# Stacked single-pass score products, decay factors spread by TensorE, and a new order list in a fused mLSTM and gated-MLP kernel

## The chip, the cores and the metric

The kernel runs on one core of one Trainium2 chip. The metric is the device time of one execution in microseconds (us), lower is better; of several executions the median counts. The engines are named as the profile names them: PE is TensorE's matmul, PEld its load of the stationary operand (the weights), DVE is VectorE, ACT is ScalarE, POOL is GpSimd, and SPq is the queue of SyncE, which here issues every DMA.

## The reference

The computation is a gated recurrent attention followed by two gated MLPs, all in fp32.

```python
B, H, S, D = 2, 8, 768, 40
for t in range(S):                                   # per batch and head
    m_new = max(f[t] + m, i[t]); f_stab = exp(f[t] + m - m_new); i_stab = exp(i[t] - m_new); m = m_new
    C = f_stab * C + i_stab * outer(v[t], k[t]);  n = f_stab * n + i_stab * k[t]
    y[t] = sigmoid(o[t]) * (C @ q[t]) / max(|n . q[t]|, 1)
x = y as [1536, 320]
x = ((x @ w_a) * (x @ w_b)) @ w_out                  # 320 -> 1536 -> 320
h = x @ w_in; out = (h * sigmoid(h)) @ w_out2        # 320 -> 2048 -> 320
```

## The kernel before, in words

**Attention.** The recurrence is cut into 12 units `u0` to `u11`: unit u is chunk c = u // 2 of 128 steps of batch b = u % 2, with all eight heads. In a unit, `scores` (parts `s0`, `s1`, four heads each) multiplies keys by queries on TensorE into a PSUM bank. The keys stand block-diagonally in `kz` (three heads of 40 rows in 120 partitions, zeros elsewhere, two buffers used in turn), so that one matmul of 120 rows against the query tile `qT` gives one head. The operands are plain fp32, and the trace shows each such matmul as two MATMUL and two LDWEIGHTS instructions.

`decays` (part `d0`) turns the forget factors, which must stand in all 128 partitions, into the triangle of decay products by a VectorE scan. In units 0 and 1 the factors are spread over the partitions by TensorE: `factors` (parts `f0`, `f1`) multiplies a column of the identity, broadcast to 128 columns, by the gate rows in `scratch`, four fp32 matmuls a part, into PSUM. In units 2 to 11, `load_fs` (parts `l2.e` and so on) reads them instead from a DRAM copy `fsd`, with a broadcasting DMA that writes 512 KB. `weigh` (`w0`, `w1`) multiplies scores by decays on VectorE, `values` (`v0`, `v1`) multiplies the result by the values on TensorE, `carried` (`car`) adds the chunk state, `update` (`upd`) with `adv_in`, `adv_old`, `adv_end` moves the state forward, and `da` to `xl` make the unit's MLP input columns in `xring`. For units below `BUSY` = 6 the state goes through six ScalarE activations and a memset a unit (`ai0` to `ai2`, `ao0` to `ao2`, `az`).

**Weights.** Twelve tiles of the first MLP (`w0` to `w11`) come as 64-bit floats in two DMAs each into a ring of four raw buffers, are narrowed on ScalarE and VectorE (`ap`, `as`, `ao`, `bp`, `bs`, `bo`), and are split into a rounded fp32r half (copies on ScalarE: `ha`, `hb`, `t0`, `t1`) and a rest (subtractions on GpSimd by the helper `rest`: `la`, `lb`, `u0`, `u1`). The tail halves cross partitions by two small DMAs (`v0`, `v1`). The second MLP's sixteen tiles (`x0` to `x15`) are made later.

**MLPs.** `first_layer` makes a hidden tile from eight fp32r matmuls of 256, 384 or 512 columns, `second_layer` three matmuls of 320 columns a unit. Passes `m0` to `m10` are the first MLP, in eleven pieces of (block of units, range of weight tiles), and `n0` to `n2` the second. A hidden tile goes through parts `a`, `b` (TensorE), `e` (eviction, ScalarE), `g` (product, VectorE, or silu, ScalarE), `h` (rounded half, ScalarE), `l` (rest, GpSimd) and `c` (TensorE).

**Order.** The string `ORDER` names every part once; the kernel runs through it, and each part appends its instructions to its engine's queue. So the list fixes the order on each engine and on SPq, each of which works strictly in its own order and waits on semaphores for data and for free buffers. Parts `f0` to `f29` are fillers, four small bf16 matmuls each on the identity (`warm`).

```python
    def scores(n):
        s = bank(f"s_u{u}", P, 4, C)
        for i in range(4):
            g, j = SLOT[4 * n + i]
            nc.tensor.matmul(out=s[:, i], lhsT=kz[u % 2][:, j, g], rhs=un["q", u][:, g], start=True, stop=True)
```

Of the kernel before, what the change touches and what calls it, by code (L numbers as in the profile page):

```python
# [32 lines left out]
lf zeros const li run0 run1 expi0 f26 f3 f8 expf0 f1 pg0 lw0.b l0.t f10 f2 f6 lw0.a w0.ap w0.bp w0.bs w0.bo w0.as  # L33
u1.f0 u0.f1 u0.f0 u0.d0 w0.t1 expf1 w0.hb l0.q l1.k l0.k u0.s0 l1.q f27 f25 l1.t u1.s0 u1.s1 lw2.b lw1.b w0.ao
starts u0.sv sel f13 w0.u1 lw2.a w0.t0 w0.u0 l2.q lw1.a w0.v0 w0.v1 w0.ha w0.la u0.d1 u1.sv u0.sk w0.lb u1.d0 f22
f16 u1.f1 u1.d1 u1.sk f28 f17 u0.s1 f15 f7 f23 f29 f21 expi1 u0.w1 f4 u0.si f12 u0.sig u1.si u0.v1 w1.bp w2.bs w1.bs
w1.bo u1.sig w2.bp u1.az w1.t1 w1.u1 w1.t0 w1.u0 w1.hb w1.lb u0.w0 u0.v0 w2.as w2.bo w2.hb f20 u0.cb f9 w2.t0 w2.u0
w2.t1 w2.ap u1.w1 u1.v1 u1.w0 prod u0.da u0.dn u1.v0 u1.cb u1.upd u1.ai1 u1.ai2 f24 u0.upd u1.ai0 u0.ai0 u1.da
u0.ai2 w2.ao u0.om w2.u1 u0.rc u0.ox u0.xt u0.ai1 w2.ha u1.dn u1.rc u1.om u1.ox w2.lb u1.xt lw5.a lw3.b pg1 u3.si
u2.ao0 l2.e u2.d0 w1.as w1.ap w1.ao u0.px u0.xh l2.k f5 f11 f18 u2.s1 u2.s0 f0 u1.px u2.si u2.car f14 u1.xh w1.ha  # L40
u2.ao1 l2.t u2.sk u2.sv u2.upd u2.w1 u2.v1 w3.bs w2.v0 l4.q lw3.a u0.az u2.ai1 u1.xl l3.e w1.v0 u0.xl w2.la m0.2.a
w3.bp w3.as u2.ai0 u2.w0 u2.v0 u2.cb w2.v1 m0.2.b w1.la u2.az w3.bo w3.hb w3.t1 w3.u1 w3.lb u3.az u3.d0 l3.k l3.q
u3.car u3.s1 u2.sig u2.cc m0.2.e m0.2.g w3.t0 u2.ai2 u2.om w3.ap w3.ao u3.cb u2.da u2.dn u2.rc m0.0.a u2.ao2 m0.0.b
m0.0.e m0.0.g w3.u0 l3.t u3.sk u3.s0 u3.w0 w1.v1 m0.1.b lw4.b w4.bs w4.bp m0.2.h w4.bo m0.1.a u3.sv u3.v0 m0.2.l
u3.w1 u3.v1 u2.ox m0.0.h m0.0.l m0.0.c w3.ha w4.t0 w4.u0 w4.t1 w4.u1 w4.hb w4.lb m0.1.e m0.1.g u3.cc u2.xt u2.px
w3.v0 lw4.a w4.as u3.upd l4.k l5.q w4.ap w4.ao u3.da u3.dn w3.la m0.3.a u3.sig u3.om u3.rc u3.ox lw5.b w5.bp w5.bs
w5.bo m0.3.e lw6.a m0.2.c w3.v1 m0.3.b m0.3.g u2.ae u4.car u4.cb u3.xt w4.ha l5.t u3.ai0 u3.px w4.v0 w4.la m0.4.a
w5.t0 u3.ai2 m0.3.h m0.3.l m0.3.c u3.xh u3.xl m0.1.h w4.v1 m0.4.b l5.k l5.e u5.d0 u3.ai1 m0.4.e m0.4.g m0.1.l m0.1.c
w5.u0 u4.s1 w5.t1 w5.u1 u2.xh u2.xl m1.0.b lw6.b w6.bp u4.si w6.bs m0.4.h m0.4.l m0.4.c u3.ao0 w5.hb w6.bo w6.hb
w6.lb w6.t0 w6.u0 w6.t1 w6.u1 u5.si l4.e u4.d0 l4.t lw7.b u4.sk u3.ao1 m1.0.a m1.0.e m1.0.g u3.ao2 m0.z1 u4.s0 u4.w0  # L50
w7.bp w7.bs w7.bo m1.1.a m1.1.e w5.lb m1.4.a lw8.b w8.bp w8.bs u5.s0 u5.sk u5.w0 w8.bo u5.s1 m1.1.b m1.1.g u4.w1
u5.w1 u3.ae u4.sv u4.v0 m1.0.h m0.z0 u5.car u5.cb u4.v1 u4.cc u5.sv u5.v1 w5.v1 w6.v1 w6.v0 w5.v0 w7.hb w8.hb w7.lb
l7.k w7.t0 w7.u0 u4.az w8.t0 m1.4.e w8.u0 w8.v0 lw9.b w7.t1 w7.u1 m1.1.h m1.1.l w8.t1 w8.lb w8.u1 w8.v1 w6.ap u5.sig
u5.v0 u5.cc u5.om w6.as w6.ao m1.4.b u4.upd m1.1.c m1.3.a u4.sig u5.da u5.dn lw10.b l6.q w7.v1 lw11.b u5.rc u4.da
# [36 lines left out]
m10.0.l y2.px y2.xh y2.xl m10.3.a m9.11.c m9.z0 lx2 x2.p x2.s x2.o x2.h x3.ho x3.lo x2.t x2.l x2.ho x2.lo m10.2.a
# [38 lines left out]
def tile_mlstm_gated_mlps(ctx: ExitStack, tc: tile.TileContext, i_gate, f_gate, q_cols, k_cols, kvo, w1, w2,  # L130
# [149 lines left out]
    def rest(eng, out_, x, hi):  # L280
        return eng.tensor_tensor(out=out_, in0=x, in1=hi.bitcast(F32), op=ALU.subtract)  # L281
# [575 lines left out]
```

## Time and profile before

| | |
|---|---|
| median of 3 runs | 464.43 us (463.83 to 472.82) |
| profiled execution: time / span | 465.23 us / 463.5 us |
| mean granted TensorE clock | 0.996 |
| PE busy | 454.5 us (98%), 3103 instructions |
| PEld / DVE / ACT / POOL busy | 435.9 / 160.7 / 219.1 / 239.2 us |
| DMA | 42.30 MB, mean 91 GB/s |

The profile covers one execution. Busy time is the time in which an engine ran an instruction, as a sum and as a share of the span. Matmuls overlap in the pipeline, so the time that a matmul costs is read from the distance of the starts of a run of them, not from its own duration (277 ns for a score matmul whose neighbours start every 112 ns).

### The profile page before, as it was taken

Reading aid. Unit: us, or ns where it says so; the run is one execution under the profiler, and the core shown is the slowest. Engines: PE = TensorE matmul, PEld = TensorE weight load, DVE = VectorE, ACT = ScalarE, POOL = GpSimd, SP = SyncE. Lnnn points to the kernel's source line nnn. Section 1 sums busy time; section 2 is a strip of 40 time slices with the busy share of each in tenths; the row PEclk is TensorE's granted clock in tenths of the full one; section 3 lists DMA queues with packets and bytes.
Section 4 is the critical chain, followed back from the end, with each engine's and each line's share of the span. In section 5 each row is a group of like instructions: output and inputs, shape, how many; then the busy total and the mean of one; then the engine's idle time right before and its main releaser. Section 6 shows DMA issues by size and latency. Waiting matters only on the chain.

```text
span 463.5 us, 7966 instructions
## 1 busy us (share of the span) xinstructions
PE 454.5 (98%) x3103; PEld 435.9 (94%) x3103; DVE 160.7 (35%) x268; ACT 219.1 (47%) x507; POOL 239.2 (52%) x278
## 2 busy tenths in 40 slices
PE   7999999999999999999999999999999999999996
PEld 6999999999999999999999999999998989998996
DVE  7876665252435465335442342314300000000000
ACT  4867777756421230232553565656634332443333
POOL 5667795666643465152443557468733343332433
PEclk9989999999999999999999999999999999999999
DMA  7887928351003241231233132133001000010001
GB/s 241 286 243 209 311 88 263 106 177 54 1 9 114 51 141 43 85 106 64 93 102 117 64 100 89 63 126 124 2 0 58 0 2 0 1 42 1 0 16 57
DMA packets 25089, 42.30 MB, mean 91 GB/s; under 512 B 2156, under 2 KB 18348, under 8 KB 25052
## 3 DMA queue, kind: packets, MB, share of 16 engines
q1 hardware_dynamic: 25052, 41.80, 28.4%
q8 instruction: 24, 0.39, 0.4%
q14 instruction: 13, 0.11, 0.1%
HBM read 38.99 MB, written 2.02 MB: 88 GB/s over the span
## 4 chain that ended last, share of the span: by engine, by line
PE 88%; DMA 7%; ACT 1%; DVE 1%; issue 1%; SPq 1%; POOL 0%; POOLq 0%; ACTq 0%
PE h L643 46%; PE acc L654 10%; PE acc L652 10%; PE acc L653 10%; PE y_u L491 4%; PE s_u L478 3%; DMA raw_j<-in_w_dram 3%; DMA e_u<-fsd 2%; PE px_u L614 1%; PE ups_u L511 1%; DMA w_j<-tl_j 1%; PE y_u L501 1%; DMA qT_u<-in_q_cols_dram 1%; DVE e_u L453 0%; SPq L230 0%
## 5 line engine op out<-in xcount | busy, mean ns | idle before, releaser
L643 PE MATMUL h<-xring,w_j 128*128 128x256 f32 (+2 forms) x1088 | 179.3, 317 | 0.1
L643 PEld LDWEIGHTS h<-xring,w_j 128*128 128x128 f32 x1088 | 161.9, 190 | 5.0 <-DMA w_j<-tl_j 0.3
L281 POOL TENSOR_TENSOR g2w<-gw,g2w 128x512 fp32r<-128x512 f32 x48 | 63.2, 1323 | 85.7 <-ACT g2w L688 83.7
L281 POOL TENSOR_TENSOR g<-g,g 128x256 fp32r<-128x256 f32 (+1 forms) x60 | 56.0, 941 | 66.6 <-ACT g L688 65.2
L281 POOL TENSOR_TENSOR w_j<-cvt_j,w_j 128x320 fp32r<-128x320 f32 (+3 forms) x72 | 62.6, 877 | 30.7 <-ACT w_j L342 13.1
L643 PE MATMUL h<-xeven,w_j 128*128 128x512 f32 x256 | 62.6, 392 | 0.0
L654 PE MATMUL acc<-w_j,g2w 128*128 128x320 f32 x192 | 59.4, 309 | 0.1
L652 PE MATMUL acc<-w_j,g2w 128*128 128x320 f32 x192 | 59.4, 310 | 0.0
L653 PE MATMUL acc<-w_j,g2w 128*128 128x320 f32 x192 | 59.3, 309 | 0.0
L688 ACT CAST g<-g 128x256 fp32r<-128x256 f32 (+1 forms) x60 | 26.6, 448 | 68.0 <-DVE g L682 46.1
L643 PEld LDWEIGHTS h<-xeven,w_j 128*128 128x128 f32 x256 | 47.1, 188 | 8.8
L684 ACT ACTIVATE gw<-h 128x512 f32<-128x512 f32 x48 | 28.5, 596 | 55.2 <-PE h L643 45.1
L682 DVE TENSOR_TENSOR g<-a,h 128x256 f32<-128x256 f32 (+1 forms) x60 | 28.2, 472 | 75.6 <-PE h L643 45.7
L652 PE MATMUL acc<-w_j,g 128*128 128x320 f32 x144 | 45.5, 316 | 0.0
L688 ACT CAST g2w<-gw 128x512 fp32r<-128x512 f32 x48 | 29.8, 621 | 32.4 <-PE acc L654 31.9
L654 PE MATMUL acc<-w_j,g 128*128 128x320 f32 x144 | 44.7, 310 | 0.3 <-POOL g L281 0.3
L653 PE MATMUL acc<-w_j,g 128*128 128x320 f32 x144 | 44.4, 308 | 0.0
L653 PEld LDWEIGHTS acc<-w_j,g2w 128*128 128x128 f32 x192 | 36.0, 188 | 1.0
L652 PEld LDWEIGHTS acc<-w_j,g2w 128*128 128x128 f32 x192 | 36.1, 188 | 1.0
L674 ACT ACTIVATE a<-h 128x256 f32<-128x256 f32 (+1 forms) x60 | 24.9, 423 | 25.6 <-PE h L643 24.8
L654 PEld LDWEIGHTS acc<-w_j,g2w 128*128 128x128 f32 x192 | 36.0, 188 | 0.4 <-POOL g2w L281 0.4
L281 DVE TENSOR_TENSOR xeven<-px_u,xeven 128x384 fp32r<-128x384 f32 x8 | 4.5, 557 | 68.5 <-ACT xeven L621 68.5
(100 smaller groups left out, 595.9 us busy)
## 6 DMA issues: line engine op xcount, KB each, us to landing
raw_j<-in_w_dram SPq DMA_DIRECT2D x16, 704.0 KB
raw_j<-in_w_dram SPq DMA_DIRECT2D x12, 512.0 KB
kvo_u<-in_kvo_dram SPq DMA_DIRECT2D x12, 480.0 KB
raw_j<-in_w_dram SPq DMA_DIRECT2D x12, 448.0 KB
e_u<-fsd SPq DMA_DIRECT2D x10, 512.0 KB
qT_u<-in_q_cols_dram SPq DMA_DIRECT2D x12, 180.0 KB
kz<-in_k_cols_dram SPq DMA_DIRECT2D x36, 60.0 KB
out_dram<-osb SPq DMA_DIRECT2D x12, 160.0 KB
```

Of the source, the lines that this page charges most:

```text
L281: return eng.tensor_tensor(out=out_, in0=x, in1=hi.bitcast(F32), op=ALU.subtract)
L478: nc.tensor.matmul(out=s[:, i], lhsT=kz[u % 2][:, j, g], rhs=un["q", u][:, g], start=True, stop=True)
L491: nc.tensor.matmul(out=T["y1"][:, h], lhsT=un["e", u][:, h], rhs=T["v"][:, h], start=True, stop=True)
L501: nc.tensor.matmul(out=y2[:, GH[g] + lo:GH[g] + G], lhsT=un["q", u][:, g], rhs=cb[:, g, lo:G], start=True, stop=True)
L643: nc.tensor.matmul(out=po, lhsT=w[:, wi * P:(wi + 1) * P], rhs=xt[:, :, xi], start=(n == 0), stop=(n == len(pairs) - 1))
L652: nc.tensor.matmul(out=o, lhsT=hi, rhs=w[:, off:off + DM], start=first, stop=False)
L653: nc.tensor.matmul(out=o, lhsT=hi, rhs=w[:, off + DM:off + 2 * DM], start=False, stop=False)
L654: nc.tensor.matmul(out=o, lhsT=lo, rhs=w[:, off:off + DM], start=False, stop=last)
L674: nc.scalar.activation(out=A[j], in_=A.pop(("p", j)), func=ACT.Copy, scale=WS ** -2)
L682: nc.vector.tensor_tensor(out=Q[j], in0=A.pop(j), in1=PB.pop(j), op=ALU.mult)
L684: nc.scalar.activation(out=Q[j], in_=PB.pop(j), func=ACT.Silu, scale=1 / WS)
L688: nc.scalar.copy(out=G2[j][:, 0], in_=Q[j])
```

## The change

1. **Stacked scores from unit 4 on** (`PLAIN = 4`). Instead of `kz`, `load_stack` fetches queries and keys (`l4.sq`, `l4.sk`, ...) into raw buffers of the weight ring in a stacked layout of 120 partitions: 40 rows of a head, its first 24 rows again, the 40 rows again, and its last 16 rows again, for nine head slots side by side (four DMAs each, 553 KB in all). `stack_high` (`hq`, `hk`) rounds each to fp32r into a two-buffer tag shared with `kz`, and `stack_low` (`lq`, `lk`) replaces 40 rows by the rests. One fp32r matmul a head then sums the three products high x low, low x high and high x high. `qT` is still loaded for `carried`; the `kz` loads of these units go.
2. **Decay factors of units 2 to 5 spread by TensorE** (`FB = 3`): they get `f0`, `f1`, `d0`, `d1` as units 0 and 1, and their four `load_fs` go.
3. **State updates**: the ScalarE form goes; units 0 to 5 use the forms of the later units, one masked multiplication on VectorE (`am`) and one on GpSimd (`ao`). `ig` moves to another pool.
4. **A new order list**, with a mark behind some parts that names the engine (`:v` VectorE, `:p` GpSimd). Of the parts of passes `m`, 31 `l` go to VectorE, 24 `e` to VectorE, 21 `h` to GpSimd and 10 `h` to VectorE; some 50 other copies, subtractions and products move as well. All 30 fillers stay; they now stand ahead of the first MLP tile.

```diff
@@ ORDER
-lf zeros const li run0 run1 expi0 f26 f3 f8 expf0 f1 pg0 lw0.b l0.t f10 f2 f6 lw0.a w0.ap w0.bp w0.bs w0.bo w0.as
...
+li lf const f29 f25 f16 f5 f22 f23 f28 zeros f10 run0 run1 expf0 expi0 pg0 f0 f4 lw0.a w0.as lw0.b f14 l1.t l0.t
...
+l4.q u3.s1 lw4.b w4.bp w3.bo w4.bs w4.bo u2.da u2.dn u2.rc w2.v0 m0.2.a w2.v1 m0.2.e w4.t1 w4.u1:v w4.t0 w4.u0 w3.hb
...
+n2.14.g n2.14.h n2.14.l n2.14.c n2.12.g n2.12.h n2.12.l n2.12.c n2.2.g n2.2.h n2.2.l n2.2.c n2.z0 n2.z1 n2.z2 n2.z3
@@
-    BUSY = 6
+    PLAIN = 4
+    FB = 3
@@
-    kz = [cat.tile([GR, G, G, C], F32, name=f"kz{i}") for i in range(2)]
+    def keys(dtype, name):
+        return at.tile([P, G * G * C], dtype, tag="kz", name=name)[0:GR].rearrange("p (j g t) -> p j g t", j=G, g=G)
+
+    kz = [keys(F32, f"kz{i}") for i in range(2)]
+    STACK = ((0, 0, D), (D, 0, KT - D), (KT, 0, D), (KT + D, KT - D, D))
+
+    def load_stack(u, x):
+        b, c, s = place(u)
+        t = raws.tile([P, G * G * C], F32, tag="raw", name=f"st{x}_u{u}")[0:GR]
+        un["st", u, x] = t.rearrange("p (j g t) -> p j g t", j=G, g=G)
+        src = (q_cols, k_cols)[x][b, c].rearrange("(j d) g t -> d j (g t)", j=G)
+        for row, lo, hi in STACK:
+            nc.sync.dma_start(out=t[row:row + hi - lo].rearrange("p (j x) -> p j x", j=G), in_=src[lo:hi])
@@
-    def rest(eng, out_, x, hi):
-        return eng.tensor_tensor(out=out_, in0=x, in1=hi.bitcast(F32), op=ALU.subtract)
+    how = {}
+
+    def copy(out_, in_):
+        e = how.get("e", "a")
+        if e == "a":
+            nc.scalar.copy(out=out_, in_=in_)
+        else:
+            (nc.vector if e == "v" else nc.gpsimd).tensor_copy(out=out_, in_=in_)
+
+    def both(out_, x, y, op):
+        (nc.vector if how.get("e") == "v" else nc.gpsimd).tensor_tensor(out=out_, in0=x, in1=y, op=op)
+
+    def rest(out_, x, hi):
+        both(out_, x, hi.bitcast(F32), ALU.subtract)
@@ chunk
         def factors(n):
-            if c > 0:
+            if c >= FB:
                 return
...
+        def stack_high(x):
+            T["sh", x] = keys(F32R, f"sh{x}_u{u}")
+            copy(T["sh", x], un["st", u, x])
+
+        def stack_low(x):
+            r = slice(x * KT, x * KT + D)
+            rest(T["sh", x][r], un["st", u, x][r], T["sh", x][r])
+
         def scores(n):
             s = bank(f"s_u{u}", P, 4, C)
+            T["s", n] = s
+            if u >= PLAIN:
+                for i in range(4):
+                    g, j = SLOT[4 * n + i]
+                    nc.tensor.matmul(out=s[:, i], lhsT=T["sh", 1][:, j, g], rhs=T["sh", 0][:, j, g],
+                                     start=True, stop=True)
+                return
...
-        def adv_old_all():
+        def adv_old():
             gbu = gb[:, b * G:(b + 1) * G, c:c + 1].to_broadcast([GR, G, G * DV])
...
-            if u < BUSY:
-                d.update(az=adv_zero, **{f"ai{j}": lambda j=j: adv_in(j) for j in range(G)})
-            else:
-                d.update(am=adv_mask)
+            d.update(am=adv_mask)
@@ mlp
-            nc.scalar.activation(out=A[j], in_=A.pop(("p", j)), func=ACT.Copy, scale=WS ** -2)
+            pa = A.pop(("p", j))
+            if how.get("e", "a") == "v":
+                nc.vector.tensor_scalar(out=A[j], in0=pa, scalar1=WS ** -2, scalar2=None, op0=ALU.mult)
+            else:
+                nc.scalar.activation(out=A[j], in_=pa, func=ACT.Copy, scale=WS ** -2)
@@ order
         for t in ORDER:
+            t, _, e = t.partition(":")
+            how.clear()
+            if e:
+                how["e"] = e
             parts[t]()
```

## Rows read from the trace of the kernel before

**Rows 1.** The page's first part: busy time, share of the span, instructions.

```profile
PE 454.5 (98%) x3103; PEld 435.9 (94%) x3103; DVE 160.7 (35%) x268; ACT 219.1 (47%) x507; POOL 239.2 (52%) x278
```

**Rows 2.** Busy time by stretch: start and end, length, each engine (instructions), clock, DMA.

```profile
0.00:34.00 34.00, 30.35 (x290) 29.63 (x291) 26.41 (x44) 22.22 (x55) 20.41 (x40) 0.95 0.82 257
34.00:70.00 36.00, 34.23 (x280) 33.17 (x279) 24.00 (x39) 26.26 (x74) 29.64 (x39) 1.00 0.65 201
70.00:452.00 382.00, 382.00 (x2490) 366.08 (x2490) 110.28 (x186) 167.00 (x373) 185.63 (x199) 1.00 0.21 67
```

**Rows 3.** PE in order of time: start, length, line, operation, count, idle before.

```profile
3.43 1.89 PE L425 MATMUL warm<-idb 128*128 128x128 bf16 x16 [3.43 <-DVE idb L727]
14.42 1.11 PE L444 MATMUL fb_u<-scratch,ident 128*128 128x128 f32 x8
15.36 0.61 PE L425 MATMUL warm<-idb 128*128 128x128 bf16 x8
33.80 1.20 PE L643 MATMUL h<-xring,w_j 128*128 128x256 f32 x8
70.50 1.20 PE L643 MATMUL h<-xring,w_j 128*128 128x256 f32 x8
78.55 6.00 PE L643 MATMUL h<-xring,w_j 128*128 128x256 f32 x48
84.39 0.31 PE L652 MATMUL acc<-w_j,g 128*128 128x320 f32 x1
```

**Rows 4.** Stretches of 2 us and one of 10, columns as in group 2.

```profile
24.00:26.00 2.00, 2.00 (x13) 1.72 (x12) 0.49 (x1) 0.84 (x3) 1.84 (x4) 0.50 0.73 218
28.00:38.00 10.00, 9.32 (x91) 9.12 (x91) 9.19 (x12) 7.86 (x22) 5.89 (x8) 1.00 0.98 278
36.00:38.00 2.00, 1.32 (x12) 1.14 (x11) 2.00 (x3) 1.53 (x6) 1.85 (x2) 1.00 0.90 257
62.00:64.00 2.00, 1.31 (x11) 1.11 (x10) 1.22 (x2) 1.75 (x4) 2.00 (x3) 1.00 0.14 33
```

**Rows 5.** The chain that ended last: start, length, what.

```profile
28.07 7.02 DMA e_u<-fsd
77.30 0.22 PE warm L425 x4
129.25 0.90 PE s_u L478 x8
148.77 0.82 PE y_u L491 x8
163.82 0.33 PE px_u L614 x3
183.65 11.17 PE h L643 x64
456.96 1.33 POOLq L852
```

**Rows 6.** Groups by line and form: busy, mean ns of one, idle before.

```profile
L478 PE MATMUL s_u<-qT_u,kz 120*128 120x128 f32 x192 | 25.1, 277 | 0.7 <-DVE e_u L485 0.7
L293 ACT CAST w_j<-cvt_j 128x512 fp32r<-128x512 f32 x12 | 7.4, 619 | 2.1 <-DVE cvt_j L276 2.1
L281 POOL TENSOR_TENSOR w_j<-cvt_j,w_j 128x512 fp32r<-128x512 f32 x12 | 15.4, 1290 | 6.9 <-ACT w_j L293 6.9
L682 DVE TENSOR_TENSOR g<-a,h 128x384 f32<-128x384 f32 x24 | 13.3, 553 | 39.4 <-PE h L643 23.5 <-ACT a L674 10.1 <-POOL g L281 4.0
L528 DVE TENSOR_TENSOR cn_u<-ups_u,bmask 120x369 f32<-120x369 f32 x4 | 2.1, 532 | 0.1
```

**Rows 7.** VectorE and GpSimd in order of time, about 225 us.

```profile
225.06 1.01 POOL L281 TENSOR_TENSOR g<-g,g 128x384 fp32r<-128x384 f32 x1 [0.88 <-ACT g L688]
225.12 1.70 DVE L256 SCALAR_TENSOR_TENSOR cvt_j<-raw_j,cvt_j 128x704 uint32<-128x704 uint32 x1
227.29 0.89 DVE L256 SCALAR_TENSOR_TENSOR cvt_j<-raw_j,cvt_j 128x704 uint32<-128x704 uint32 x1
```

More of the change, by code (lines that the diff above doesn't have):

```diff
@@ L38 @@
[L38 to L42, printed above, removed]
@@ L309, in tail_lo @@
                 B["tl"] = cvt.tile([P, P], F32R, tag="tl", name=f"tl_j{j}")
-            rest(nc.gpsimd, B["tl"][p], B["c"][p, 0:P], W[1, j][p, s_])
+            rest(B["tl"][p], B["c"][p, 0:P], W[1, j][p, s_])
         def tail_move(n):
@@ L369, in tile_mlstm_gated_mlps @@
     fs, mm = carve(scratch[1], S, S + 1)
-    ig = at1.tile([BH, S], F32, tag="ig", name="ig")
+    ig = gp.tile([P, 2, S // 2], F32, tag="g2", name="ig", bufs=2)[0:BH].rearrange("p n t -> p (n t)")
     f0, gs = fg, mm[:, 0:S]
@@ L447, in decays @@
         def decays(n):
-            h = slice(4 * n, 4 * n + 4) if c == 0 else slice(0, H)
-            if c > 0 and n == 1:
+            h = slice(4 * n, 4 * n + 4) if c < FB else slice(0, H)
+            if c >= FB and n == 1:
                 return
             e = un["e", u][:, h].rearrange("p h t -> p (h t)")
-            f = T["f", n].rearrange("p h t -> p (h t)") if c == 0 else e
+            f = T["f", n].rearrange("p h t -> p (h t)") if c < FB else e
             nc.vector.tensor_tensor_scan(out=e, data0=f, data1=ident8[:, h].rearrange("p h t -> p (h t)"),
@@ L517, in adv_tile @@
             return T["cn"]
-        def adv_zero():
-            nc.gpsimd.memset(adv_tile()[:, 2, 0], 0.0)
-        def adv_in(j):
-            n = G if j else 2
-            nc.scalar.activation(out=adv_tile()[:, 0:n, j], in_=T["ups"][:, 0:n, j], func=ACT.Copy,
-                                 scale=mask[0:GR, j:j + 1])
         def adv_mask():
@@ L553, in combine @@
             if c == 0:
-                nc.scalar.copy(out=y, in_=T["y1"])
+                copy(y, T["y1"])
             else:
@@ L562, in gate_out @@
         def gate_out():
-            nc.gpsimd.tensor_tensor(out=un["o", u], in0=un["o", u], in1=T["y"][:, :, 0:D], op=ALU.mult)
+            both(un["o", u], un["o", u], T["y"][:, :, 0:D], ALU.mult)
         def magnitudes():
@@ L583, in chunk @@
                  px=lambda: x_product(1, u, T["x"]), xh=lambda: x_high(1, u), xl=lambda: x_low(1, u), d0=lambda: decays(0))
-        if c == 0:
+        if u >= PLAIN:
+            d.update({f"h{'qk'[x]}": lambda x=x: stack_high(x) for x in range(2)})
+            d.update({f"l{'qk'[x]}": lambda x=x: stack_low(x) for x in range(2)})
+        if c < FB:
             d.update(f0=lambda: factors(0), f1=lambda: factors(1), d1=lambda: decays(1))
-        else:
+        if c > 0:
             d.update(car=carried, cc=combine_add)
@@ L589, in chunk @@
             d.update(sk=scale_k, upd=update)
-            if u < BUSY:
-                d.update(az=adv_zero, **{f"ai{j}": lambda j=j: adv_in(j) for j in range(G)})
-            else:
-                d.update(am=adv_mask)
+            d.update(am=adv_mask)
             if c > 0:
-                d.update(ae=adv_end)
-                if u < BUSY:
-                    d.update({f"ao{g}": lambda g=g: adv_old(g) for g in range(G)})
-                else:
-                    d.update(ao=adv_old_all)
+                d.update(ae=adv_end, ao=adv_old)
         return d
@@ L625, in x_low @@
         xt = x_columns(m, blk)[:, n]
-        rest(nc.vector, xt[:, 3:6], px.pop(u), xt[:, 0:3])
+        nc.vector.tensor_tensor(out=xt[:, 3:6], in0=px.pop(u), in1=xt[:, 0:3].bitcast(F32), op=ALU.subtract)
     PAIRS = {
@@ L687, in high @@
             G2[j] = hidden(m, "g2", 2)[:, :, 0:nt]
-            nc.scalar.copy(out=G2[j][:, 0], in_=Q[j])
+            copy(G2[j][:, 0], Q[j])
         def low(j):
-            rest(nc.gpsimd, G2[j][:, 1], Q.pop(j), G2[j][:, 0])
+            rest(G2[j][:, 1], Q.pop(j), G2[j][:, 0])
         def three(j):
@@ L723, in constants @@
         nc.vector.memset(mm[:, 0:1], NEG)
-        nc.gpsimd.memset(scratch[1][:, 0:C], 0.0)
+        nc.gpsimd.memset(scratch[1][:, 0:FB * C], 0.0)
         make_identity(nc, ident)
@@ L770, in tile_mlstm_gated_mlps @@
         parts.update({f"u{u}.{n}": f for n, f in ch[u].items()})
-        for n, f in (("q", load_q), ("k", load_k), ("t", load_kvo)):
+        for n, f in (("q", load_q), ("t", load_kvo)):
             parts[f"l{u}.{n}"] = lambda f=f, u=u: f(u)
-        if u >= B:
+        if u < PLAIN:
+            parts[f"l{u}.k"] = lambda u=u: load_k(u)
+        else:
+            parts.update({f"l{u}.s{'qk'[x]}": lambda u=u, x=x: load_stack(u, x) for x in range(2)})
+        if u >= FB * B:
             parts[f"l{u}.e"] = lambda u=u: load_fs(u)
```

214 lines of the change are left out of this document (107 added, 107 removed).

## The prediction

> **What bounds the kernel now.** I read the busy times first. TensorE works in 98% of the span and no other engine in more than 52% [rows 1]. The busy times by stretch come next: from 70 to 452 us PE is busy in all 382.00 us, at full clock [rows 2]. In that stretch nothing that another engine does can be gained or lost unless it becomes so late that PE waits; only PE's own work counts. What is lost lies ahead of it. I measure it at one point, the sixteenth first-layer group. It starts at 70.50 us [rows 3]. What PE had to do before it, at full rate, is 57.9 us: from the order list, 15 first-layer groups at 0.96, five second-layer groups at 0.88, twelve score parts at 0.90, twelve value parts at 0.82, four spreading parts at 0.90, 29 fillers at 0.22, and some 8.5 us of small parts (the prices follow below). So **12.6 us** are lost by 70.5 us. 3.4 of them are the start: PE's first instruction waits for the identity until 3.43 us [rows 3]. Some 2.6 go to the half clock of the first matmuls: the first sixteen filler matmuls start 0.11 us apart [rows 3], where four of them take 0.22 us at full rate [rows 5], and the spreading that follows starts slow too. The rest is waiting, of which the trace shows the large pieces: the clock at 0.50, which is 1.2 of 2.4 GHz, in 24 to 26 us, after a stretch of short value matmuls and a wait; and PE busy only 1.32 and 1.31 us of 2 at 36 and 62 us [rows 4]. The first of these two follows a decay load that holds the chain for 7.02 us [rows 5]. The DMA engines are 0.82 busy up to 34 us [rows 2] and 0.98 in 28 to 38 us [rows 4]: the opening is held by transfers, with VectorE behind them at 9.19 of 10 us [rows 4].
>
> **PE's own work: two terms that nearly cancel.** The prices are distances of starts. A first-layer matmul of 256 columns costs (84.39 - 78.55) / 48 = 0.122 us [rows 3], one of 384 columns 11.17 / 64 = 0.175 [rows 5]. A plain fp32 score part of four heads is eight instructions (192 for 96 matmuls [rows 6]) and costs 0.90 us [rows 5].
>
> *Removed:* sixteen score parts, 16 x 0.90 = 14.4 us. *Added in their place:* 64 fp32r matmuls of 128 columns, a shape this trace does not have. From below, the line through 256 and 384 columns gives 0.122 - 0.053 = 0.069 each. From above, a matmul that costs what the old pair did gives 0.225. Between them stand the rows in which the weight load, and not the streaming, must be the limit: a value part with 41 columns takes 0.82 / 8 = 0.103 an instruction, and a transpose of one fp32 pass 0.33 / 3 = 0.110 [rows 5]. Both load 128 columns of 4-byte weights, as the stacked scores do, so I take 0.106: 6.8 us, a saving of **7.6** (9.97 at 0.069; nothing at 0.225). The Trainium skill, "TensorE: Matmul & The Clock Gate", section "LDWEIGHTS (loading the stationary operand)", puts a load at P / 1.2 ns, 107 ns for 128 columns, which agrees with the value row; by that the saving would be 7.6. The same page's "Back-to-back issue gap" gives 81 ns for load and matmul pairs at N = 128; by that it would be 9.2. No row here shows 81 ns for 4-byte weights.
>
> *Added:* `f0`, `f1` of units 2 to 5, eight parts of eight fp32 instructions. The nearest row is the same operation: from 14.42 to the next start at 15.36 us it is 0.94 with its neighbours' gaps [rows 3]; the score part of the same shape is 0.90. 8 x 0.90 = **7.2** (7.5 at 0.94). The fillers cost the same 30 x 0.22 [rows 5]. PE's work changes by -0.4 us (-2.8 to +7.5).
>
> **The opening.** By the new list PE has 62.1 us of work ahead of the sixteenth group, 4.2 more than before (eight more spreading parts; two value parts, four old score parts and others fall later), so work that ran later at full density now stands where PE waited. *Transfers:* four decay loads of 512 KB go, the 7.02 us chain with them; four stacks of 553 KB come for units 4 and 5, instead of two key loads of 180 KB and one or two decay loads later. The sum to this point is about equal, but up to the first MLP group it is some 10% larger (two stacks, one more unit's inputs). Before, that group started at 33.80 us [rows 3]; I expect 36 to 38, with 33 us of PE work done instead of 26. SPq also issues four DMAs a stack instead of three a key tile; each waits behind the one before for its raw buffer, and weight loads and `v0`, `v1` queue behind.
> *ScalarE* loses some 8 us here (state activations, moved parts) and is no limit. *GpSimd:* each stack rest of 1152 columns costs by its 512-column row [rows 6] 1.29 x 1152 / 512 = 2.9 us; four of them are in the opening, and 5 us in all are added to the 50.0 that it had [rows 2]. A rounded stack on ScalarE is 0.62 x 1152 / 512 = 1.4 us [rows 6].
> *VectorE* gets the most: 22 items up to the sixteenth group (four masks at 0.53, four MLP rests, two evictions and twelve others of 256 to 384 columns at 0.42 to 0.55 [rows 6]), 9.6 us, less 1.4 for attention that comes later: +8.2. It had 26.41 + 24.00 = 50.4 busy before 70 us [rows 2], so 58.6 now.
>
> How much of the 12.6 remains? The floor is the start and the cold clock. The start shrinks by about 0.8, since the memset of `kz` no longer stands ahead of the identity: 2.6 + 2.6 = 5.2. VectorE sets the other end: at the share that it kept up to 34 us, 26.41 / 34 = 0.777 [rows 2], 58.6 us take 75.4, a loss of 13.3. I take **9.5**, nearer the middle: VectorE would be at 58.6 / 71.6 = 0.82, between that 0.78 and the 0.92 of its densest ten us [rows 4]. The gain is 12.6 - 9.5 = **3.1 us**, with -0.7 to 7.4 as ends.
>
> **After 70 us.** Stacks of units 6 to 11 (twelve loads of 553 KB in some 130 us) meet DMA engines that are 0.21 busy, and VectorE's moved subtractions meet 110 of 382 us busy [rows 2]; I cost them at nothing, and 1 to 2 us if a rounded stack is late for its scores, which wait in PE's queue ahead of everything else. At the end PE waits for the last rest on GpSimd, 1.33 us [rows 5], of which a fourth second-layer group now covers a part: 0.3.
>
> **Sum.** The profiled execution took 465.23 us, 1.7 more than its span and 0.8 above the median of 464.43. 465.2 - 3.1 - 0.4 - 0.3 = 461.4; against the median, **460.6**.
>
> **Rivals.**
> *VectorE bounds the opening (slower).* For it: the 0.777 share, and row 225.12 us, where a two-input VectorE instruction took 1.70 us instead of 0.89 because a GpSimd subtraction had begun 0.06 us earlier [rows 7]. Thirteen of the moved items have two inputs in SBUF; GpSimd is busy 50 of 70 us [rows 2], so each meets half of a 1 us subtraction seven times in ten: 13 x 0.35 = 4.5 us more on VectorE. Then 63.1 / 0.777 = 81 us, a loss of 19: 6.4 more than before, less 0.7: 470. Without the blocking it is 464.4. It decides from a VectorE time of 74.7 us to the sixteenth group. Against it: VectorE ran at 0.92 for 10 us when it was wanted. I price it at 467, the middle. The Trainium skill, "SBUF — State Buffer", section "Who interferes with whom", says that such an instruction and a GpSimd one that reads SBUF block each other for a whole instruction; row 225.12 agrees, and that rule speaks against the change.
> *The fp32r score costs what fp32 did, so the first part does not do what it says.* +7.6: 468.2. For it: no fp32r matmul under 256 columns is in the trace; against it: both known shapes lie on one line.
> *All goes well.* Loss of 5.2 to 6.5 and 0.069 a score matmul: 460.6 - 3.6 - 2.4 = 454.6.
> *Only the PE work changes, waits are as long as before:* 463.7; it lies within my range.
>
> **Numbers.** Forecast with a loss of 7 to 12 and its neighbour, nothing gained: 0.65, 457.5 to 464.4. VectorE-bound: 0.17. fp32r no faster: 0.06. All well: 0.10. Two or three things late together: 0.02. The range cuts half of the good end and the upper half of the slow ones: 455.5 to 467.5. Two per cent, which is about what a measurement tells from no change, is 455.1 and 473.7: faster 0.10, slower 0.03, same 0.87.
>
> **What would show it.** Score parts of units 4 on at 0.42 us by their starts (0.28 or 0.90 say that the price was wrong); eight new spreading parts at 0.9; the sixteenth group near 71.6 us; no decay load in the chain before it; VectorE at 0.82 up to there; PE busy without gaps after. The prediction is wrong if PE waits beyond 80 us, if the clock falls again in the opening, or if the sixteenth group starts before 69 or after 75 us.

## The result: 1.2% slower, and where the profile after shows it

The changed kernel takes 469.11 us in the median of its runs (468.27 to 470.38), the kernel before 464.13 beside it: a ratio of 1.0119, 95% interval 1.0091 to 1.0146. A later set gave 1.0092 (1.0063 to 1.0120). The forecast was 460.6 us, with 467.5 as the upper end of its range. The profiled execution took 468.87 us, with a span of 467.2, against 465.23 and 463.5 before: the two traces differ by 3.7 us.

The busy times of the page come first, then those of the three stretches of [rows 2], with the same columns:

```profile
PE 454.9 (97%) x3103; PEld 437.1 (94%) x3103; DVE 217.6 (47%) x386; ACT 197.7 (42%) x411; POOL 227.9 (49%) x266
```

```profile
0.00:34.00 34.00, 30.16 (x297) 29.43 (x298) 26.47 (x46) 19.01 (x41) 20.14 (x45) 0.95 0.70 225
34.00:70.00 36.00, 31.11 (x249) 30.81 (x248) 22.80 (x46) 18.21 (x43) 22.91 (x28) 0.91 0.59 162
70.00:452.00 382.00, 382.00 (x2491) 366.07 (x2491) 168.35 (x296) 154.74 (x318) 179.51 (x191) 1.00 0.29 88
...
39.00:41.00 2.00, 0.01 (x1) 0.00 (x0) 1.96 (x3) 0.84 (x2) 1.04 (x1) 0.96 1.00 221
41.00:43.00 2.00, 0.00 (x0) 0.00 (x0) 0.19 (x1) 0.00 (x0) 1.92 (x2) 0.50 0.75 176
43.00:45.00 2.00, 1.55 (x7) 1.58 (x8) 0.00 (x0) 0.00 (x0) 0.45 (x1) 0.50 0.13 43
45.00:47.00 2.00, 2.00 (x12) 2.00 (x10) 0.76 (x3) 1.17 (x3) 0.00 (x0) 0.50 0.02 4
```

PE's own sum is what it was (454.9 for 454.5 us), and after 70 us it is busy in all 382.00, as in [rows 2]. The loss lies between 34 and 70 us: PE is busy 31.11 us there and not 34.23, at a mean granted clock of 0.91 and not 1.00. The rows of 2 us narrow it down. PE does nothing from 39 to 43 us, then works at a clock of 0.50, which is 1.2 GHz, up to 47. Between 41 and 43 us VectorE and ScalarE idle with it (0.19 and 0.00 us) and only GpSimd works, while the DMA engines are busy at 0.75. PE waits for a transfer, as the rows below show; ScalarE waits for another, the load of a weight tile, for 5.19 us up to 45.03; VectorE waits for ScalarE. From 43 us on the DMA engines have next to nothing to move (0.13, 0.02).

PE in order of time, columns as in [rows 3], names PE's transfer and the bill:

```profile
2.65 3.60 PE L453 MATMUL warm<-idb 128*128 128x128 bf16 x32 [2.65 <-DVE idb L755]
...
36.23 1.06 PE L472 MATMUL fb_u<-scratch,ident 128*128 128x128 f32 x8
37.13 1.88 PE L531 MATMUL y_u<-vx_u,e_u 128*128 128x41 f32 x16
43.45 3.75 PE L519 MATMUL s_u<-qT_u,kz 120*128 120x128 f32 x16 [4.44 <-DMA qT_u<-in_q_cols_dram]
...
46.85 3.48 PE L667 MATMUL h<-xring,w_j 128*128 128x256 f32 x24
50.17 1.05 PE L472 MATMUL fb_u<-scratch,ident 128*128 128x128 f32 x8
50.98 1.20 PE L667 MATMUL h<-xring,w_j 128*128 128x256 f32 x8
...
78.17 2.13 PE L667 MATMUL h<-xring,w_j 128*128 128x256 f32 x16
```

PE waits 4.44 us for the queries of unit 3. The sixteen score matmuls behind the wait then need 46.85 - 43.45 = 3.40 us where two parts cost 1.80 at full clock [rows 5], and the first three MLP groups 50.17 - 46.85 = 3.32 where 24 x 0.122 is 2.93 [rows 3]: 2.0 us for the half clock. The first MLP group starts at 46.85 us (33.80 before, forecast 36 to 38). The sixteenth, counted by matmuls, starts at 78.17; it started at 70.50 before, and I had forecast 71.6. So 6.6 us are missing against the forecast, and wait and half clock together are 6.4 us.

What held the queries is in SP's queue. Here are SP's issues in order of time, with start, length (waiting included), line, operation, transfer and count.

```profile
29.43 1.47 SPq L220 DMA_DIRECT2D st_u<-in_k_cols_dram  x4
31.18 4.76 SPq L220 DMA_DIRECT2D st_u<-in_q_cols_dram  x4
36.46 0.94 SPq L204 DMA_DIRECT2D qT_u<-in_q_cols_dram  x2
37.96 0.35 SPq L246 DMA_DIRECT2D raw_j<-in_w_dram  x1
38.40 12.11 SPq L342 DMA_DIRECT2D w_j<-tl_j  x4
```

And the chain that ended last, as in [rows 5], has these pieces in this stretch and right behind it:

```profile
29.43 7.01 DMA st_u<-in_k_cols_dram
36.46 6.86 DMA qT_u<-in_q_cols_dram
...
43.45 3.75 PE s_u L519 x16
...
63.66 0.40 PE s_u L514 x4
```

The two stacks of unit 5, eight DMAs and 1.1 MB, are issued at 29.43 and 31.18 us, and SP spends 4.76 us on the second of them, waiting. Only then come the queries of units 3 and 4. Unit 3's are wanted at 39 us and land 6.86 us after their issue, behind the stacks' bytes. Unit 5's stacks are first used by its scores at 63.66 us. Work that is due 24 us later stands ahead of work that is due now. The decay load of 7.02 us that held the old chain [rows 5] is gone, as forecast; a stack of 7.01 us has its place.

The two lists have the prices. A stacked score part takes 0.40 us, 0.100 a matmul (forecast 0.106 and 0.42). A new spreading part takes 0.81 to 0.90 us at full clock, from its start to the next (50.98 - 50.17, 37.13 - 36.23; forecast 0.90). Three of the eight stand in an earlier stretch of half clock (the last section has it) and take 31.60 - 27.20 = 4.40 us together. The Trainium skill, "TensorE: Matmul & The Clock Gate", section "LDWEIGHTS (loading the stationary operand)", gives P / 1.2 ns, 107 for 128 columns, near the measured 100, which decides here. The 81 ns of that page's "Back-to-back issue gap" is not reached here with 4-byte weights.

### The profile page after: what moved, and what is told of

Same layout as the page of the kernel before. It is cut to its first block, busy times and chain, and to the rows that moved or that the text cites. A ratio compares the mean times of both kernels' runs of the same rounds, so it can differ in the third digit from the quotient of the medians.

```text
span 467.2 us, 8049 instructions
## 1 busy us (share of the span) xinstructions
PE 454.9 (97%) x3103; PEld 437.1 (94%) x3103; DVE 217.6 (47%) x386; ACT 197.7 (42%) x411; POOL 227.9 (49%) x266
## 4 chain that ended last, share of the span: by engine, by line
PE 88%; DMA 7%; ACT 2%; SPq 1%; issue 0%; DVE 0%; POOL 0%; ACTq 0%; POOLq 0%
PE h L667 47%; PE acc L678 10%; PE acc L676 10%; PE acc L677 10%; PE y_u L531 3%; PE px_u L638 2%; DMA st_u<-in_k_cols_dram 2%; DMA qT_u<-in_q_cols_dram 1%; DMA w_j<-tl_j 1%; PE s_u L514 1%; DMA kvo_u<-in_kvo_dram 1%; PE s_u L519 1%; PE y_u L541 1%; DMA kz<-in_k_cols_dram 1%; PE ups_u L551 1%; ACT w_j L301 0%
## 5 line engine op out<-in xcount | busy, mean ns | idle before, releaser
L667 PE MATMUL h<-xring,w_j 128*128 128x256 f32 (+2 forms) x1088 | 181.5, 317 | 0.4 <-DMA w_j<-tl_j 0.4
L306 POOL TENSOR_TENSOR w_j<-cvt_j,w_j 128x320 fp32r<-128x320 f32 (+3 forms) x66 | 53.0, 809 | 36.7 <-ACT w_j L301 34.6
L306 POOL TENSOR_TENSOR g<-g,g 128x256 fp32r<-128x256 f32 (+1 forms) x29 | 28.5, 982 | 30.3 <-ACT g L301 15.7
L301 ACT CAST w_j<-cvt_j 128x320 fp32r<-128x320 f32 (+3 forms) x68 | 29.0, 452 | 26.3 <-DVE cvt_j L272 13.2
L702 ACT ACTIVATE a<-h 128x256 f32<-128x256 f32 (+1 forms) x36 | 14.9, 417 | 36.0 <-PE h L667 30.1
L303 POOL CAST g<-g 128x256 fp32r<-128x256 f32 (+1 forms) x21 | 12.3, 588 | 30.9 <-DVE g L710 18.1
```

The source lines that it names most:

```text
L301: nc.scalar.copy(out=out_, in_=in_)
L303: (nc.vector if e == "v" else nc.gpsimd).tensor_copy(out=out_, in_=in_)
L306: (nc.vector if how.get("e") == "v" else nc.gpsimd).tensor_tensor(out=out_, in0=x, in1=y, op=op)
L667: nc.tensor.matmul(out=po, lhsT=w[:, wi * P:(wi + 1) * P], rhs=xt[:, :, xi], start=(n == 0), stop=(n == len(pairs) - 1))
L702: nc.scalar.activation(out=A[j], in_=pa, func=ACT.Copy, scale=WS ** -2)
```

## The experiments

The question was which of the following put 6 us into the opening. **A**: the stacks' place in SP's queue, ahead of transfers that are due sooner; in the form A1 the number of DMAs is what delays, in A2 their bytes. **B**: VectorE, with 8 us of work moved to it, as the rival of the prediction has it. **C**: one of the two parts of the change isn't worth its price. Where an experiment changes the order, the diff shows the list's entries, `-` where they were, `+` where they are.

**1. Unit 3's queries ahead of the stacks.**

```
- u1.xl l5.sk u5.hk l5.sq u5.lk u5.f1 ... u3.d0 l3.q u3.s0
+ u1.xl l3.q l5.sk u5.hk l5.sq u5.lk u5.f1 ... u3.d0 u3.s0
```

> The changed kernel with one part moved: the query load of unit 3 (l3.q) is issued ahead of unit 5's key stack instead of behind both stacks. Theory A (the opening is lost on SPq: unit 3's query load stands behind eight stack DMAs, is issued at 36.46 us and lands at 43.31, and PE waits 4.44 us and then runs some 5 us at 1.2 GHz): the wait and the half clock go, 4.4 + 2.2 us less, 462 to 465 us. Theory B (VectorE bounds the opening, the prediction's slower rival): PE waits as long for something else, 468 to 470 us.

Measured: 1.0045 (1.0002 to 1.0088), 468.29 us. The wait for the queries is gone, and the next one is there. From the waits of PE (line, releaser: total, times, longest) and from the chain:

```profile
PE h L666 <- DMA w_j<-tl_j: 3.8, 1, 3.8
```

```profile
38.36 6.36 DMA w_j<-tl_j
```

A move of 32 KB that completes weight tile 2 is issued at 38.36 us behind the stacks and takes 6.36 us to land; PE stands before the first MLP group instead of before the scores. On this chip the kernel before takes 465.72 us, 1.6 more than in the first set. With that taken off, the time lies between A's range and B's; what PE waits for is a transfer and not VectorE. So the queries alone are too little to move: the wait passes to whatever is due next behind the stacks.

**2. One DMA a stack instead of four.** The rows of both stacks stand in another order, the same one for queries and keys.

```
- src = (...)[x][b, c].rearrange("(j d) g t -> d j (g t)", j=G)
- for row, lo, hi in STACK: nc.sync.dma_start(out=t[row:row + hi - lo]..., in_=src[lo:hi])
+ src = (...)[x][b, c].unsqueeze(1).to_broadcast([GR, G, G, C])
+ nc.sync.dma_start(out=t.rearrange("p (j g t) -> p j g t", j=G, g=G), in_=src)
```

> The changed kernel in its own order, each stack fetched by one DMA of the same 553 KB instead of four (the rows come in another order, so the scores are other numbers). Theory A1 (number: each DMA waits for the one issued eight before it, so the eight of unit 5's stacks hold unit 3's query load back until the first of them lands): that load is issued at about 32 us instead of 36.46 and lands at 36 to 38, PE waits under 1 us, 463 to 465.5 us. Theory A2 (bytes: the load lands when the 1.1 MB ahead of it have been moved, however many DMAs they are): it lands within 1.5 us of 43.3, 468 to 469.5 us. Theory B: 468 to 470 us.

Measured: 1.0059 (1.0028 to 1.0091), 468.26 us. From SP's issues and the chain:

```profile
31.34 0.39 SPq L219 DMA_DIRECT2D st_u<-in_k_cols_dram  x1
33.10 0.36 SPq L219 DMA_DIRECT2D st_u<-in_q_cols_dram  x1
33.51 3.00 SPq L204 DMA_DIRECT2D qT_u<-in_q_cols_dram  x2
```

```profile
33.51 9.70 DMA qT_u<-in_q_cols_dram
```

```profile
PE s_u L518 <- DMA qT_u<-in_q_cols_dram: 2.4, 1, 2.4
```

The queries land when they did in the changed kernel (33.51 + 9.70 = 43.21 us for 36.46 + 6.86 = 43.32), but in this execution the whole opening is 1.9 us late already ahead of the stacks (the first is issued at 31.34 us for 29.43). So times are counted from the first stack's issue. In the changed kernel's two traces, the one above and that of experiment 11, the queries are issued 7.03 and 8.80 us after it and land 13.89 and 13.92 us after it: an issue 1.8 us later does not move the landing, as A2 says. With one DMA a stack they are issued 2.17 us after it and land 11.87 us after it, 2.0 us sooner, and PE waits 2.41 us instead of 4.44. A1 expected less than 1. So the bytes hold the larger part, 2.4 us of the wait; 2.0 us go with the number of the DMAs or their form, as far as one trace of this kernel tells. Part of that is lost again: PE waits 1.96 us for a weight tile at 59 us (0.45 in the changed kernel). The ratio lies below both of the changed kernel's, and its interval overlaps that of 1.0092.

**3. Both stacks of unit 5 and the steps on its key stack moved behind `w0.v0`,** which is behind unit 3's queries and weight tile 2.

```
- u1.xl l5.sk u5.hk l5.sq u5.lk u5.f1 ... u3.d0 l3.q ... w2.v0 ... w0.v0 m0.0.a
+ u1.xl u5.f1 ... u3.d0 l3.q ... w2.v0 ... w0.v0 l5.sk u5.hk l5.sq u5.lk m0.0.a ...
```

> The changed kernel with unit 5's stacks (both loads, the rounded keys and the key rests) moved behind the first MLP groups' small weight moves (after w0.v0), 14 parts later; its scores are needed only at 63 us. Theory A: PE's wait of 4.44 us goes, and the tail moves of weight tile 2, which the first MLP group needs, go out earlier too: 460.5 to 463.5 us. Theory B: 468 to 470 us. If the stacks only shift the wait to unit 5: 465 to 468 us.

Measured: 0.9970 (0.9943 to 0.9997), 464.48 us for 465.72. With the same 1.6 us taken off, the time lies within A's range. PE has neither wait. PE in order of time:

```profile
40.62 3.12 PE L666 MATMUL h<-xring,w_j 128*128 128x256 f32 x24
...
53.99 0.41 PE L677 MATMUL acc<-w_j,g 128*128 128x320 f32 x1 [1.35 <-POOL g L305]
...
72.47 2.13 PE L666 MATMUL h<-xring,w_j 128*128 128x256 f32 x16
```

The sixteenth group starts at 72.47 us, 5.7 sooner than in the changed kernel and 0.9 behind the forecast; the first MLP group starts at 40.62, 6.2 sooner, but still 2.6 behind the forecast. So the place of the stacks is the cause of the wait. One wait of 1.35 us is new, for a rest on GpSimd.

**4. The stacked scores alone, in the kernel before, from unit 6 on** (their rests on VectorE, and loads and preparation steps put in at places that I chose by hand).

```
+ PLAIN = 6
- l6.k ... l11.k
+ l6.sk l6.sq u6.hk u6.lk u6.hq u6.lq ... (units 6 to 11)
```

> The kernel before, with the first part of the change alone and only where PE works without a gap: stacked single-pass scores for units 6 to 11, rests on VectorE, the rest of the order as it was (u7.s1 and u7.w1 moved to just ahead of u7.car; the gate tile in the pool that the change uses). Twelve score parts at 0.40 instead of 0.90 us. If a score part's saving is a pure saving of PE's work after 70 us: 6.0 us less than before, 457 to 459 us. If the loads, the rounding or the rests are late for the scores: 460 to 463 us.

Measured: 1.0217 (1.0153 to 1.0281), 475.88 us. The groups of VectorE by form (busy, mean ns, idle before) and the waits of PE:

```profile
L295 DVE TENSOR_TENSOR sh_u<-st_u,sh_u 40x1152 fp32r<-40x1152 f32 x12 | 16.9, 1409 | 10.5 <-ACT sh_u L490 10.4
```

```profile
PE y_u L520 <- DVE e_u L514: 4.2, 3, 2.3
```

VectorE stands idle 10.4 us before these rests, with other work queued behind them, since ScalarE has not rounded the stack; PE then waits for VectorE's products. Both expectations are missed by more than 10 us. This says nothing against the stacks. It says that the place of each step in its engine's queue can cost more than the part brings. It is a poor test of the part by itself; experiment 7 is the better one.

**5. Order of 3, and the decay factors of units 4 and 5 from device memory again.**

```
- FB = 3
+ FB = 2
- u5.f0 u5.f1 u5.d1 ... u4.f0 u4.f1 u4.d1
+ w0.v0 l5.e l5.sk ...        + u3.v0 l4.e m0.1.b ...
```

> The kernel e3_stacks_late with the decay factors of units 4 and 5 loaded from DRAM again (two loads of 512 KB after w0.v0 and u3.v0), those of units 2 and 3 still spread by TensorE. Four spreading parts of 0.96 us go. Theory A (PE's work is what counts once the opening is past, and these four parts stand where PE no longer waits): 3.8 us less than e3, ratio to before 0.997 - 0.008 = 0.989. Theory C (the opening is held by SPq and transfers up to 70 us, so two more loads cost what the spreading saved): within 1 us of e3.

Measured: 1.0118 (1.0038 to 1.0198), 470.98 us, though PE has four spreading parts less to do. The chain, and ScalarE in order of time:

```profile
41.74 5.33 DMA st_u<-in_k_cols_dram
```

```profile
47.24 1.15 ACT L300 CAST sh_u<-st_u 120x1152 fp32r<-120x1152 f32 x1 [4.00 <-DMA st_u<-in_k_cols_dram]
```

The decay load of 512 KB stands ahead of the stacks, so these land later; ScalarE waits 4.00 us for one, and the MLP's activations are queued behind that. PE waits 3.3 and 2.0 us for second-layer inputs. Neither expectation fits: by the two ratios the kernel takes 6.9 us more than that of experiment 3.

**6. Order of 3, part 2 undone: units 2 to 5 all from device memory.**

```
- FB = 3
+ FB = 1
```

> The kernel e3_stacks_late with all of units 2 to 5 loaded from DRAM again, so the second part of the change undone (loads of 512 KB after u0.v1, u1.v0, w0.v0 and u3.v0). Eight spreading parts go, 7.7 us of PE's work. Theory A: units 2 and 3 stand in the stretch that transfers hold, so their loads give back what their parts cost (two loads of about 2 us each and a chain of 7 us as in the kernel before): 0.5 us slower to 3 us slower than e5, ratio 0.990 to 0.996. If transfers did not bound the opening: 3.8 us faster than e5, ratio 0.981.

Measured: 1.0178 (1.0095 to 1.0261), 474.18 us. The waits of PE:

```profile
PE y_u L540 <- DMA qT_u<-in_q_cols_dram: 6.0, 1, 6.0
PE h L666 <- DMA w_j<-tl_j: 2.6, 1, 2.6
```

PE saves some 7 us of spreading and waits longer than that. In this order, with the loads where I put them, the spreading on PE is worth its price, and I had expected the loads to lose far less. (The places were chosen by hand, and the best ones may lose less: the kernel before had these loads and is faster than this one. So what part 2 is worth by itself stays open.)

**7. Order of 3, part 1 undone: plain fp32 scores throughout.**

```
- PLAIN = 4
+ PLAIN = 12      (l*.sk, l*.sq, u*.hk, u*.lk, u*.hq, u*.lq become l*.k)
```

> The kernel e3_stacks_late with the first part of the change undone: plain fp32 scores in all units, keys block-diagonal as before, no stacks, no rounding and no rests of them (query loads of units 5 and 6 and the key load of unit 8 moved to where they are needed). 16 score parts at 0.90 instead of 0.40 us are 8.0 us more PE work. If the stacks cost nothing but PE's time there: 8.0 us more than e3, ratio 1.014. If the stacks' 8.8 MB, their 16 ScalarE and 16 rest instructions still hold PE somewhere: 4 to 7 us more.

Measured: 1.0130 (1.0062 to 1.0199), 471.68 us. The page's busy times:

```profile
PE 460.7 (98%) x3167; PEld 442.9 (94%) x3167; DVE 205.1 (44%) x376; ACT 182.8 (39%) x397; POOL 203.4 (43%) x258
```

PE has 460.7 us of work where the kernel of experiment 3 has 452.8. By the two ratios to the kernel before, the stacked scores are worth about 1.6% of the time, 7.4 us, by the two intervals give or take 3.4 (the two ran on different chips); sixteen parts at 0.90 - 0.40 are 8.0.

**8. Order of 3, without the marks that put work on other engines.**

```
- w4.u1:v u2.xt:p u3.sk:v ...
+ w4.u1 u2.xt u3.sk ...
```

> The kernel e3_stacks_late with every engine mark off, so that all copies are on ScalarE and all subtractions on GpSimd as in the kernel before (some 45 us leave VectorE). Theory B (VectorE holds the opening): faster than e3 by 1 to 3 us. Theory A (VectorE does not hold it; the marks relieve ScalarE and GpSimd): slower than e3 by 1 to 8 us, with PE waiting for GpSimd or ScalarE before 230 us.

Measured: 1.0593 (1.0514 to 1.0672), 492.87 us. The busy times and the longest sum of PE's waits:

```profile
PE 463.9 (95%) x3103; PEld 440.8 (90%) x3103; DVE 164.7 (34%) x278; ACT 226.9 (46%) x493; POOL 277.7 (57%) x292
```

```profile
PE acc L674 <- POOL g L302: 9.7, 8, 4.3
```

VectorE is relieved of 55 us, and the kernel takes 29 us more than that of experiment 3, where A had 1 to 8. Most of this lies behind the opening and tells nothing of B: from 70 to 452 us PE is busy 366.02 us of 382. In the opening VectorE works 46.19 us before 70 instead of 56.02, and the sixteenth group starts at 75.89 us, 3.4 later; PE waits there for GpSimd (1.90 us at 54.90). Since the work taken off VectorE went to GpSimd and ScalarE, this alone does not rule B out. Experiment 3 does: it leaves VectorE's work as it was, and the sixteenth group starts 5.7 us sooner.

**9. Order of 3, and the rest of unit 5's query stack behind the rest of the MLP product that PE waited for** in experiment 3.

```
- m0.0.e u5.lq m0.0.b m0.0.g m0.0.h m0.0.l u3.upd
+ m0.0.e m0.0.b m0.0.g m0.0.h m0.0.l u5.lq u3.upd
```

> The order with late stacks (e3_stacks_late), and unit 5's rest of the query stack (2.87 us on GpSimd) put behind the rest of the product m0.0 instead of ahead of it. Left after the stacks are moved is a wait of 1.35 us at 54 us, in which TensorE waits for that product's rest on GpSimd. Theory (the part that GpSimd's queue order cost): the wait goes, the sixteenth first-layer group starts at 71.1 instead of 72.5 us, the kernel takes 1.0 to 1.4 us less, 0.994 of the kernel before. Rival (the rest is needed soon by the scores of unit 5, 57 us): the wait moves to those scores, nothing gained.

Measured: 0.9967 (0.9946 to 0.9989), 463.11 us for 465.13. PE in order of time, and the stretch up to that point, columns as in [rows 2]:

```profile
71.86 2.13 PE L666 MATMUL h<-xring,w_j 128*128 128x256 f32 x16
```

```profile
0.00:71.86 71.86, 68.11 (x612) 66.83 (x612) 58.09 (x102) 43.41 (x98) 49.99 (x75) 0.98 0.73 219
```

The wait of 1.35 us is gone (0.31 and 0.25 are left nearby), and the sixteenth group starts 0.6 us sooner, not 1.35. The ratio does not tell this kernel from that of experiment 3; the profiled spans, 460.8 and 461.5, are 0.7 apart. It is the fastest version found, a little under both kernels.

**10. As 9, with the decay factors of units 4 and 5 loaded behind the stacks, and unit 5's scan late.**

```
- w0.v0 l5.sk u5.hk l5.sq u5.lk m0.0.a ... u5.f0 u5.d0
+ w0.v0 l5.sk u5.hk l5.sq u5.lk l5.e m0.0.a ... u5.d0 lw6.b
```

> As e9_low_late, with the decay factors of units 4 and 5 from device memory, as in the kernel before (two loads of 512 KB, unit 5's behind both stacks, its scan shortly before its scores' eviction and no longer right behind the load). TensorE has four spreading parts of 0.95 us less. If the loss of e5_fb2 (+14 us of waits) came from the scan standing in VectorE's queue ahead of the MLP's work, this one gains nearly the 3.8 us: 0.986 to 0.990. If the bytes are too many there, waits for transfers appear again before 60 us and it is slower than e9_low_late.

Measured: 1.0119 (1.0083 to 1.0155), 471.14 us. SP's issues and PE's longest wait:

```profile
42.34 7.50 SPq L236 DMA_DIRECT2D e_u<-fsd  x2
49.95 0.54 SPq L341 DMA_DIRECT2D w_j<-tl_j  x1
```

```profile
PE h L666 <- DMA w_j<-tl_j: 5.7, 1, 5.7
```

The expectation laid the loss of experiment 5 on the scan in VectorE's queue; with the scan late the loss is the same, so that was wrong or not enough. The second case came: here the two loads hold SP for 7.50 us, mostly because their tiles are still in use (3.4 us for PE's value matmuls, 3.2 for VectorE's product), and the tail moves of the next weight tile are issued behind them: PE waits 5.7 us. The chain that ended last runs through unit 5's query stack, which lands at 48.21 us, and ScalarE behind it, and reaches SP at 51.22 us, just when SP gets there by its own queue. Which of the two is worth more is not shown. Either way a transfer that is due stands behind others, as in the changed kernel.

**11. The changed kernel once more, beside 9 and 10.**

> The changed kernel as it is, beside the two others on one chip. Expected 1.009 to 1.013 of the kernel before, the 4.4 us wait for unit 3's queries at 43 us and a half clock behind it. If it comes out at 1.000 the loss was the other chip's.

Measured: 1.0092 (1.0063 to 1.0120), 469.62 us. On this chip experiment 9 stands at 0.9967 (0.9946 to 0.9989), and the intervals don't touch: moving five entries of the list is worth some 1.2%, 6 us.

## Why the prediction was wrong, step by step

- **PE's own work** was right. Score parts take 0.40 us (0.42 forecast), spreading parts 0.81 to 0.90 at full clock (0.90). Three spreading parts ran at half clock and cost 4.40 us instead of 2.70; the clock had fallen in the kernel before too, a little earlier and on other work [rows 4]. Experiment 7 puts the whole of part 1 at about 7.4 us, give or take 3.4, for a forecast of 7.6.
- **The opening** is the step that failed, and in it the transfers. I wrote that their sum was "about equal" and that "weight loads and `v0`, `v1` queue behind" the stacks, and gave the latter no price. The sums came out as forecast: by mean rate and time 9.6 MB up to the first MLP group for 8.7 before, and 15.8 MB up to the sixteenth for 16.1. What decides is not the sum but the order of bytes against the time at which each is due, and for some 2 us of the wait the number or form of the DMAs (experiment 2). Unit 5's stacks, due at 63.66 us, are ahead of queries that are due at 39. The rows that I had would have given the price: a load of 512 KB held the chain for 7.02 us while the DMA engines were 0.98 busy [rows 4, 5]. Two stacks of twice that in sum, right ahead of the queries, could have been read from the new list as a wait of that size.
- **The loss of 9.5 us** before the sixteenth group was a value between a floor and VectorE's share, with no term for a due transfer. In the changed kernel it is 78.17 - 62.1 = 16.1. With the stacks moved and the rest on GpSimd put later (experiment 9) it is 71.86 - 62.1 = 9.8. That is near the 9.5, and what I left out is 6.3 us on top. The 9.5 was a choice between two ends, though, and its nearness is in part luck: the first MLP group comes 2.5 us behind its forecast even there (40.47 us).
- **The clock.** I listed a second fall in the opening as a sign that the forecast is wrong. It came in the wait of 4.44 us, and cost 2.0. In experiments 1 and 2 a fall to 0.50 came with waits of 3.77 and 2.41 us too, and by the same reckoning cost 1.5 and 1.4. The wait of 1.35 us in experiment 3 has none with it (1.00 from 52 to 56 us).
- **VectorE** has 58.09 us up to the sixteenth group in experiment 9, a share of 0.81; forecast were 58.6 and 0.82. After the identity at the start, none of PE's longer waits there is for VectorE. In the changed kernel itself VectorE is only 55.65 us busy up to there, a share of 0.71, since it waits with the others. The rival that it bounds the opening falls by this and by experiment 3, though its side, slower, was the right one.
- **The rival of the fp32r price** falls with 0.40 us a part, and "only the PE work changes" with the new wait.
- **After 70 us**: no wait of PE, as forecast. From the sixteenth group to the end the kernel takes 467.2 - 78.17 = 389.0 us; before it took 393.0. The forecast had 4.9 us less, the traces show 4.0. Of these 0.9 us 0.3 are the gain that I forecast for the very end: PE idles 3.59 us of the last 11.5 before and 3.56 now, so it did not come. The rest I have not assigned.
- **The sum.** Without the wait and its half clock the change brings 0.3% (0.1 to 0.5), some 1.5 us, where I forecast 3.8. The profiled executions differ by 2.7 us. So the repaired kernel falls short of the forecast too, by 1.1 to 2.3 us, and only part of that is found.

What is shown: the place of the stacks costs some 6 us (experiments 3, 9 and 11), and part 1 is worth its price (7). What rests on one trace: that 2.4 us of the wait go with the stacks' bytes and 2.0 with the number or form of their DMAs (2). What is open: the worth of part 2, since its loads never stood at their best places (5, 6 and 10). What is only argued: that the half clock from 43 to 47 us is due to the wait before it. It came with each of the three waits above, but the clock also falls without one (last section).

## What to carry to other kernels

When a list of work is reordered, write beside each transfer the time at which its first reader wants it, and look for a large early one ahead of a small late one; the sum of bytes and the busy shares say nothing on that. A wait that goes away by moving one transfer passes to the next due one behind the same blocker (experiment 1), so move the blocker. And a stretch of steps that wait on one engine's queue (a rounding, a scan, a load whose buffer is still in use) delays all that is queued behind it, whatever it saves elsewhere (experiments 4, 5 and 10).

## What the runs showed of the hardware that was not expected

- A stacked fp32r matmul of 128 columns with its own weights takes 0.100 us, near the 0.103 of the 41-column values [rows 5] and below the 0.122 of 256 columns. Three times the columns of the values cost no more, so the columns do not set it here; I take it to be the load of the weights.
- A DMA of 180 KB needs 5.12, 6.86 or 9.70 us from issue to landing when 1.1 MB were issued just ahead, and a move of 32 KB 6.36 us. In the changed kernel's two traces the 180 KB are issued 7.03 and 8.80 us after the first stack DMA and land 13.89 and 13.92 us after it. With two stack DMAs instead of eight they land 11.87 us after it.
- The granted clock can fall to 0.50 with PE busy throughout. In the changed kernel PE works 2.00 of 2 us in each of these, and the clock is low in the second; what went before it are value matmuls of 41 columns, and ten matmuls of 16 and twelve of 6 columns at 25 to 27 us. The columns are those of [rows 2]:

```profile
24.00:26.00 2.00, 2.00 (x24) 1.88 (x23) 1.02 (x3) 1.99 (x6) 0.00 (x0) 1.00 0.41 75
...
28.00:30.00 2.00, 2.00 (x11) 2.00 (x11) 2.00 (x5) 1.51 (x4) 1.86 (x4) 0.50 1.03 291
```
